# Sliding-window attention beside a gated GeLU block: bursts of maxima moved by a slot, and one gate/up tile moved from the attention's filler to the stage of seven products

## The chip, the cores and the metric

The kernel runs on one core of a Trainium2 chip. The metric is the device time of one execution in microseconds (us). Three runs of the kernel before gave 1066.36, 1067.74 and 1068.19 us, so the median is 1067.74. The profile shows one further execution.

## What is computed

The input x has 2048 tokens of 640 numbers. It is normalised, and two blocks read the result; both outputs are added to x. Everything is float32 at the interface.

```python
x = A_x
xn = _layernorm(x, axis=-1)
return x + _A_ref(xn, A_wqkv, A_wo) + _B_ref(xn, B_w_gate, B_w_up, B_w_down)
```

Block A is attention with 32 heads of 20 numbers. A query sees itself and the 255 keys ahead of it; softmax runs over those. Block B is `(gelu(xn @ w_gate) * (xn @ w_up)) @ w_down` with 1728 hidden columns.

## The kernel before

**Precision.** A dense product of float32 matrices is made of three products of a high and a low part (high by high, low by high, high by low). With 640 = 5 x 128 input rows, one 128x512 block of output takes 15 matrix products of 512 columns (`dense_steps`, L105).

**Stages.** They follow each other on TensorE: (1) layer norm, transposes and the first q/k and v projections; (2) the attention, in which TensorE fills the time between attention steps with projections, which the text calls the filler; (3) the gate/up products that the filler did not do, in pairs of token blocks with a scheme of seven products in place of eight (`gate_up_pair`, L935), ahead of them four plain blocks of the last, half-width tile (`gate_up`, L105 with tile `ps_g`); (4) the down and output projections (`terms`, L1202).

**Gate/up tiles.** The hidden columns are cut into 14 tiles (0 to 13) of 128 gate and 128 up columns; tile 13 has 64 of each. Tiles 0 to NFA-1 go through the filler (`gate_up_fill`): 4 token chunks of 512, a gate and an up block each, 15 products a block, so 120 products a tile. Tiles NFA to 12 go through `gate_up_pair`: a call does two of the four chunks of a tile with 6 + 9 + 6 + 9 + 6 + 9 + 9 = 54 products, so 108 products a tile. In both cases the result `he` is stored to DRAM as `hd`, from where stage 4 loads it.

**The attention's clock.** `attention()` walks through units u of four heads and 512 queries (32 units, and a 33rd turn for the last one's end). Each unit has NS = 14 slots, and in each slot the code writes down, in this order: actions that fell due (`tick`), two maxima (`pull_max`) in some slots, in slot 0 the weighted sum of values of the unit before (`av_unit`, L586, tile `ps_o`), in odd slots up to 11 two pieces of scores with their exponentials (`exp_piece`, matrix products L545 into `ps_e`, exponential L547 on ScalarE), and RATE/14 products of the filler (`pull_fill`; a v product of 320 columns counts 0.65). All engines but SyncE keep the order in which this is written.

**Maxima.** `max_pair` computes scores once more in another orientation, as 60x64 tiles of the array (L480, tile `ps_m`; 8 to 16 products for a pull of two), and VectorE takes the row maximum (L490, `junk`). Eight pairs make one unit's maxima: in the kernel before four in slot 0 (two ahead of `av_unit`, two behind it), two in slot 4 and two in slot 8; the first turn takes slot 2 for the second pair. MXD slots after a unit's last pair `max_end` transposes the maxima with one product (L507, `ps_n`), and a DMA writes them into rows of the queries, so that the scores come out with the maximum already taken off.

**After the scores.** GpSimd zeroes what lies outside the window in the exponentials P (`clear`, L558 and L561), then `av_unit` uses them. The scores have two PSUM buffers (tag "ex", which `av_unit` uses too), the maxima four ("mx"), the filler two ("dn"). P has three buffers a unit, called X, Z and Y in the order of their exponentials; `av_unit` reads X first, Y last.

**The filler's order** is the list `sets`: first the third and last chunk of q/k pair 0, then the sets one after the other, each with four chunks. A q/k chunk is saved by `save_qk` in steps on ScalarE (L265, L246), VectorE (L261) and GpSimd (L247), then stored to DRAM; a gate/up chunk takes five steps on ScalarE and VectorE and none on GpSimd. The weights of the next set are split into high and low on ScalarE (L622) and GpSimd (L627). When the slot number reaches V1_SLOT, the filler does the v projection of the upper 16 heads (`proj_v`, tile `ps_v`).

```python
sets = [("qk", 1), ("gu", 0), ("qk", 2), ("qk", 3), ("qk", 4)]
sets += [("gu", f) for f in range(1, NFA)] + [("gu", NF - 1)]
```

The filler does all of `sets` but the last; what is left when the slots end is done behind the last `av_unit`.

Of the kernel before, what the change touches and what calls it, by code (L numbers as in the profile page):

```python
# [28 lines left out]
SR = 3 * DH  # L29
QROWS = 64 + SR  # L30
NS = 14
RATE = 42.2
V1_SLOT = 158
MXD = 6
KSLOT = 9
LAG = 3, 5, 4, 4, 4, 4, 3, 3, 4, 3, 2, 1, 1, 1
NFA = 6
HD = D // 2
HR = 5
NQD = 9  # L40
# [25 lines left out]
def block_kernel(ctx, tc, x, wqk, wv, wgu, wdo, wdl, out):  # L66
# [131 lines left out]
    def at(slot, fn, *a):  # L198
        acts.setdefault(slot, []).append((fn, a))
# [9 lines left out]
    def flush():  # L209
        while lates:  # L210
            fn, a = lates.pop(0)
            fn(*a)
# [108 lines left out]
    def run(*gens):  # L321
        for gen in gens:
            for _ in gen:
                pass
# [121 lines left out]
    def load_stack(u, which=(0, 1)):  # L446
        g, c = divmod(u, NC)
        for m in range(80 * g // 128, (80 * g + 79) // 128 + 1):
            assert all((m + 5 * i, c) in done for i in which), (u, m)

        for i in which:
            dst, src, top, again = ((qs[u % NQ], qd[c], 1, 2), (ks[u % NK], kd[c], 0, 0))[i]
            for j in (0, 2):
                for p, part, n in ((j * 32, top, 2), (j * 32 + 2 * DH, again, 1), (64 - j * 32, 0, 3)):
                    nc.sync.dma_start(dst[p:p + DH * n, j:j + 2].rearrange("p j t -> p (j t)"),
                                      src[g, part:part + n].rearrange("s (d j) t -> (s d) (j t)",
                                                                      j=4)[:, j * C:(j + 2) * C])
# [73 lines left out]
    def exp_piece(u, s):  # L531
        g, c = divmod(u, NC)
        bi, j = divmod(s, 4)
        bank = pieces(c)[bi]
        q = qs[u % NQ]
        if j == 0:
            pts[u, bi] = ap.tile([128, 4, C], F32, name="P", tag="P", bufs=3)
        pt = pts[u, bi]
        lo = min(p[1] for p in bank)
        hi = max(p[1] + p[3] for p in bank)  # L540
        ps = psx.tile([128, C], F32, name="ps_e", tag="ex")
        for kb, col, q0, n in sorted(bank, key=lambda p: p[3]):
            k = ks[(u - (kb < 4 * c)) % NK]
            kc = kb % 4 * 128
            nc.tensor.matmul(ps[:, col:col + n], k[0:QROWS, j, kc:kc + 128], q[0:QROWS, j, q0:q0 + n],  # L545
                             start=True, stop=True)
        nc.scalar.activation(pt[:, j, lo:hi], ps[:, lo:hi], AF.Exp, scale=SCALE)  # L547
        if j == 3:
            defer(1, clear, u, bi)
# [56 lines left out]
    def load_gu(f):  # L606
        raws = []
        for i in range(2 if f < NF - 1 else 1):
            raw = wrp.tile([128, KT, 128], F32, name="wr", tag="wr")
            nc.sync.dma_start(raw, wgu[2 * f + i])  # L610
            raws.append(raw)
        return raws
# [4 lines left out]
    def split_later(pool, bufs, raw):  # L617
        hi = pool.tile([128, KT, 128], F32R, name="wqh", tag="wqh", bufs=bufs)
        lo = pool.tile([128, KT, 128], F32R, name="wql", tag="wql", bufs=bufs)

        def high():
            nc.scalar.activation(hi, raw, AF.Copy)  # L622
            for k in range(KT):
                defer(1 + k, low, k)

        def low(k):
            nc.gpsimd.tensor_tensor(out=lo[:, k], in0=raw[:, k], in1=hi[:, k].bitcast(F32), op=OP.subtract)  # L627

        defer(1, high)
        return hi, lo  # L630
# [37 lines left out]
                                   lambda k: xh[:, k, cs], lambda k: xl[:, k, cs], KT)  # L668
            defer(1, *((late, c4) if i else (c1,)))

    sets = [("qk", 1), ("gu", 0), ("qk", 2), ("qk", 3), ("qk", 4)]
    sets += [("gu", f) for f in range(1, NFA)] + [("gu", NF - 1)]
    pools = (wp, None), (hp, 2)
    rest = []

    def filler():
# [6 lines left out]
        for s, (kind, i) in enumerate(sets[:-1]):  # L683
            nxt = []
            after = sets[s + 1]
            for c in range(NC):
# [14 lines left out]
                if c in (1, 2) and c <= len(raws):  # L701
                    nxt.append(split_later(*pools[(s + 1) % 2], raws[c - 1]))
                if pending and now[0] >= V1_SLOT:
                    pending = False
# [8 lines left out]
    def x_sums(p, k, half):  # L713
        w = C // 2
        a, b = (slice((2 * p + i) * C + half * w, (2 * p + i) * C + half * w + w) for i in (0, 1))
        eh, el = xh.bitcast(F32), xl.bitcast(F32)
        live = {}

        def tile_of(i):
            live[i] = ap.tile([128, w], F32, name="tx", tag="tx")  # L720
            return live[i]

        def pool(o, i, j, op):
            nc.gpsimd.tensor_tensor(out=o, in0=i, in1=j, op=op)

        def store(i):
            t = live[i]
            defer(2, lambda: nc.sync.dma_start(td[p][i][:, k, half * w:half * w + w], t))

        def s1():  # L730
            pool(tile_of(1), eh[:, k, b], eh[:, k, a], OP.subtract)

        def s2():
            pool(live[1], live[1], el[:, k, b], OP.add)

        def s3():
            pool(live[1], live[1], el[:, k, a], OP.subtract)
            store(1)

        def s4():  # L740
            pool(tile_of(2), eh[:, k + 2, b], live[1], OP.subtract)

        def s5():
            pool(live[2], live[2], el[:, k + 2, b], OP.add)
            store(2)

        def s6():
            pool(tile_of(4), eh[:, k + 2, a], live[2], OP.subtract)

        def s7():  # L750
            pool(live[4], live[4], el[:, k + 2, a], OP.add)
            store(4)

        def s8():
            pool(tile_of(3), eh[:, k + 2, b], eh[:, k, b], OP.subtract)

        def s9():
            pool(live[3], live[3], el[:, k + 2, b], OP.add)

        def s10():  # L760
            pool(live[3], live[3], el[:, k, b], OP.subtract)
            store(3)

        return s1, s2, s3, s4, s5, s6, s7, s8, s9, s10
# [6 lines left out]
    def pull_max(n, slot):  # L771
        for _ in range(n):
            x = next(stream, None)
            if x is None:
                return
            max_pair(*x)
            if x[1] == 7:
                at(slot + (MXD if slot >= 0 else 4), max_end, x[0])

    def tick():  # L780
        todo = [y for t in sorted(t for t in acts if t <= now[0]) for y in acts.pop(t)]
        return sorted(todo, key=lambda y: y[0] is max_end)

    def pull_fill(n):
        debt[0] += n
        while debt[0] > 0:
            debt[0] -= next(fill, 1.0)

    def attention():
        now[0] = -1  # L790
        load_stack(0)
        load_stack(1)
        load_stack(2)
        for i, (p, k, half) in enumerate((p, k, half) for p in range(NC // 2) for k in range(2) for half in range(2)):
            for j, fn in enumerate(x_sums(p, k, half)):
                at(XS0 + XSN * i + 2 * j, fn)
        for i in range(12):
            now[0] = i - 13
            for fn, a in tick():
                fn(*a)  # L800
            if i % 2 == 0:
                pull_max(2, now[0])
            flush()
            pull_fill(2 * RAMP)
        pull_fill(GAP)
        for u in range(NU + 1):
            for i in range(NS):
                T = now[0] = NS * u + i
                for fn, a in tick():
                    fn(*a)  # L810
                if i in (0, 4, 8) or T == 2:
                    pull_max(2, T)
                if i == 0 and u:
                    av_unit(u - 1)
                    flush()
                    pull_max(2, T)
                if i % 2 and i < 12 and u < NU:
                    exp_piece(u, i - 1)
                    if i == 1 and u:
                        pull_fill(1)  # L820
                        debt[0] -= 1
                    exp_piece(u, i)
                flush()
                if u + 3 < NU and i in (KSLOT, 12):
                    load_stack(u + 3, (int(i == KSLOT),))
                pull_fill(RATE / NS)
        while acts:
            now[0] += 1
            for fn, a in tick():
                fn(*a)  # L830
            flush()
        now[0] = None
        run(fill)
        assert not acts
# [446 lines left out]
    order.__enter__()  # L1281
    raws_w = load_gu(NFA)
    banks = [psg.tile([128, C], F32, name="ps_g", tag=f"g{i}") for i in range(4)]
# [32 lines left out]

    raws_next = {NFA + 1: load_gu(NFA + 1)}
    for j, f in enumerate(range(NFA, NF - 1)):
        end = f + 1 == NF - 1
# [93 lines left out]
    for n, (p, k) in enumerate(steps):  # L1413
        i = n % (NQD + 1)
# [71 lines left out]
```

## Time and profile before

| what | value |
|---|---|
| the profiled execution's own time | 1067.07 us |
| its span, first to last instruction of the profile | 1065.2 us |
| median of three runs without a profile | 1067.74 us |
| TensorE busy | 1052.9 us, 99% of the span |
| VectorE, ScalarE, GpSimd busy | 68%, 50%, 35% |
| attention, first `av_unit` to last filler product | 108.5 to 637.9 us |
| plain blocks of tile 13 | 637.92 to 651.55 us |
| stage 3, 7 tiles, 756 products | 651.55 to 822.94 us |
| stage 4 | 822.94 to the end |

Times are counted from the first instruction of the profile. A row of the timeline gives the start, the length to the end of the last of the merged instructions, the engine, the line, the operation, the tiles (output first), the shape and the count; the bracket behind it is the idle time ahead and what ended it. Matrix products overlap, and their ends are modelled, so the text works with distances from start to start. PE is TensorE, PEld its weight loads, DVE VectorE, ACT ScalarE, POOL GpSimd, SP SyncE.

### The profile page before, as it was taken

Reading aid. Unit: us, or ns where it says so; the run is one execution under the profiler, and the core shown is the slowest. Engines: PE = TensorE matmul, PEld = TensorE weight load, DVE = VectorE, ACT = ScalarE, POOL = GpSimd, SP = SyncE. Lnnn points to the kernel's source line nnn. Section 1 sums busy time; section 2 is a strip of 40 time slices with the busy share of each in tenths; the row PEclk is TensorE's granted clock in tenths of the full one; section 3 lists DMA queues with packets and bytes.
Section 4 is the critical chain, followed back from the end, with each engine's and each line's share of the span. In section 5 each row is a group of like instructions: output and inputs, shape, how many; then the busy total and the mean of one; then the engine's idle time right before and its main releaser. Section 6 shows DMA issues by size and latency. Waiting matters only on the chain.

```text
span 1065.2 us, 25614 instructions
## 1 busy us (share of the span) xinstructions
PE 1052.9 (99%) x9429; PEld 832.7 (78%) x9429; DVE 722.9 (68%) x1985; ACT 531.1 (50%) x1120; POOL 375.6 (35%) x550
## 2 busy tenths in 40 slices
PE   8999999999999999999999999999999999999998
PEld 8877666666678766666666678888888999999998
DVE  7845656565554456666666627787776879888887
ACT  4434665566656565565656565332234543433332
POOL 6021665777764484746556351211100000000000
PEclk9999999999999999999999999999999999999999
DMA  5642344455452244424333215565766873343433
GB/s 196 187 150 75 105 148 131 137 141 176 135 157 81 84 143 122 147 90 139 99 105 123 66 63 199 173 247 204 251 247 247 277 254 129 128 134 103 133 129 105
DMA packets 105190, 158.74 MB, mean 149 GB/s; under 512 B 15420, under 2 KB 60092, under 8 KB 105064
## 3 DMA queue, kind: packets, MB, share of 16 engines
q1 hardware_dynamic: 102680, 150.95, 44.0%
q10 hardware_dynamic: 2384, 6.16, 1.7%
q8 instruction: 74, 1.21, 0.5%
q14 instruction: 52, 0.43, 0.1%
HBM read 101.78 MB, written 54.92 MB: 147 GB/s over the span
## 4 chain that ended last, share of the span: by engine, by line
PE 84%; DVE 5%; POOL 4%; DMA 3%; issue 2%; ACT 2%; SPq 0%; ACTq 0%; DVEq 0%; POOLq 0%
PE ps_d L105 25%; PE ps L1202 19%; PE ps_g L935 16%; PE ps_e L545 7%; PE ps_v L105 6%; PE ps_o L586 5%; PE ps_m L480 4%; PE ps_g L105 1%; POOL pt L247 1%; DVE junk L490 1%; DMA xi<-x 1%; POOL P L561 1%; POOL P L558 1%; DVE ss L1040 1%; DMA hr<-od 1%
## 5 line engine op out<-in xcount | busy, mean ns | idle before, releaser
L490 DVE CUSTOM_DVE_ANT_0 junk<-ps_m,mask 128x320 bf16<-128x320 f32 (+2 forms) x512 | 243.0, 475 | 171.7 <-PE ps_m L480 114.1
L547 ACT ACTIVATE P<-ps_e 128x512 f32<-128x512 f32 (+2 forms) x384 | 199.0, 572 | 106.3 <-PE ps_e L545 102.2
L1202 PE MATMUL ps<-wb,at 128*128 128x320 f32 x999 | 156.1, 309 | 0.3 <-DVE at L1040 0.3
L1202 PEld LDWEIGHTS ps<-wb,at 128*128 128x128 f32 x999 | 148.9, 188 | 0.8 <-DVE at L1040 0.6
L105 PE MATMUL ps_d<-xh,wql 128*128 128x512 f32 x430 | 136.7, 421 | 0.0
L105 PE MATMUL ps_d<-xh,wqh 128*128 128x512 f32 x430 | 135.1, 419 | 0.0
L105 PE MATMUL ps_d<-xl,wqh 128*128 128x512 f32 x430 | 134.8, 418 | 0.0
L545 PE MATMUL ps_e<-qs,ks 124*128 124x128 bf16 (+2 forms) x704 | 118.2, 279 | 0.3
L558 POOL TENSOR_SCALAR_AFFINE_SELECT P<-P 128x512 f32<-128x512 f32 x128 | 82.2, 642 | 101.9 <-ACT P L547 99.5
L545 PEld LDWEIGHTS <-ks 124*128 124x128 bf16 x704 | 48.6, 99 | 61.0 <-issue 48.6
L1202 PE MATMUL ps<-wt,at 128*128 128x320 f32 x552 | 89.2, 310 | 0.8 <-DVE xr L1225 0.8
L105 PEld LDWEIGHTS ps_d<-xl,wqh 128*128 128x128 f32 x430 | 77.4, 189 | 15.4 <-issue 3.4
L105 PEld LDWEIGHTS ps_d<-xh,wql 128*128 128x128 f32 x430 | 77.0, 189 | 15.7 <-issue 3.6
L105 PEld LDWEIGHTS ps_d<-xh,wqh 128*128 128x128 f32 x430 | 76.7, 189 | 15.5 <-issue 3.1
L1202 PEld LDWEIGHTS ps<-wt,at 128*128 128x128 f32 x552 | 82.9, 188 | 1.3 <-DVE xr L1225 1.0
L561 POOL TENSOR_SCALAR_AFFINE_SELECT P<-P 128x512 f32<-128x512 f32 x112 | 70.8, 642 | 35.4 <-ACT P L547 35.4
L1156 ACT ACTIVATE at<-ss 128x512 fp32r<-128x512 f32 x59 | 37.3, 633 | 88.5 <-DVE ss L1040 88.5
L586 PE MATMUL ps_o<-P,v 64*32 64x320 f32 (+4 forms) x2816 | 75.9, 348 | 0.9 <-POOL P L561 0.6
L247 POOL TENSOR_TENSOR pt<-r,pt 128x512 bf16<-128x512 f32 x40 | 46.5, 1164 | 77.1 <-ACT pt L246 73.7
L586 PEld LDWEIGHTS ps_o<-P,v 64*32 64x32 f32 x2816 | 48.5, 106 | 26.6 <-POOL P L558 3.4
L480 PE MATMUL ps_m<-ks,qs 60*64 60x320 bf16 (+3 forms) x1472 | 63.3, 260 | 2.6 <-DVE xl L192 1.1
L480 PEld LDWEIGHTS <-qs 60*64 60x64 bf16 x1472 | 28.3, 105 | 42.1 <-issue 36.7
(195 smaller groups left out, 1754.0 us busy)
## 6 DMA issues: line engine op xcount, KB each, us to landing
hr<-hd SPq DMA_DIRECT2D x104, 128.0 KB
hd<-he SPq DMA_DIRECT2D x50, 256.0 KB
wr<-wgu SPq DMA_DIRECT2D x27, 320.0 KB
qs<-qd SPq DMA_DIRECT2D x64, 120.0 KB
ks<-kd SPq DMA_DIRECT2D x64, 120.0 KB
xi<-x SPq DMA_DIRECT2D x16, 320.0 KB
qs<-qd SPq DMA_DIRECT2D x64, 80.0 KB
ks<-kd SPq DMA_DIRECT2D x64, 80.0 KB
```

The lines of the kernel that those rows point to most:

```text
L105: nc.tensor.matmul(ps, a(k), b(k), start=n == 0, stop=n == 3 * nk - 1)
L247: nc.gpsimd.tensor_tensor(out=pt[:, l, :], in0=r, in1=pt[:, 1, :], op=OP.subtract)
L480: nc.tensor.matmul(ps[64 * h:64 * h + 64, col:col + w], q[rows, j, q0:q0 + 64], ks_, start=True, stop=True, tile_position=(64 * r, 64 * h))
L490: nc.vector.tensor_tensor_reduce(out=junk[:, 0:n], in0=ps[:, 320 - n:320], in1=mask[:, 320 - n:320], scale=1.0, scalar=NEG, op0=OP.add, op ...
L545: nc.tensor.matmul(ps[:, col:col + n], k[0:QROWS, j, kc:kc + 128], q[0:QROWS, j, q0:q0 + n], start=True, stop=True)
L547: nc.scalar.activation(pt[:, j, lo:hi], ps[:, lo:hi], AF.Exp, scale=SCALE)
L558: nc.gpsimd.affine_select(out=a, in_=a, pattern=[[0, 4], [1, 128]], compare_op=OP.is_ge, fill=0.0, base=0, channel_multiplier=-1)
L561: nc.gpsimd.affine_select(out=a, in_=a, pattern=[[0, 4], [-1, 128]], compare_op=OP.is_ge, fill=0.0, base=-1, channel_multiplier=1)
L586: nc.tensor.matmul(os[r][32 * j:32 * j + 32, qa:qb], v[rows, w0_:w0_ + 32], pt[rows, j, col + qa - q0:col + qb - q0], start=r not in begun ...
L935: nc.tensor.matmul(ps, i, j, start=first and n == 0, stop=n == len(work) - 1, skip_group_check=True)
L1156: nc.scalar.activation(hi[:, 3:7], s, AF.Copy)
L1202: nc.tensor.matmul(ps[bank][:, 0:HD], *work[bank][j], start=bank not in begun, stop=final[p, bank] == n and j == len(work[bank]) - 1, skip ...
```

## The change

NFA goes from 6 to 5, so tile 5 goes through `gate_up_pair` and no longer through the filler; RATE, the filler products of a unit, goes from 42.2 to 38.8. The pulls of maxima in slots 4 and 8 move to slots 5 and 9 (in the first turn 2 to 3), which are slots with scores; MXD goes from 6 to 7, so `max_end` also falls into a slot with scores. In the list of sets q/k pairs 2 and 3 go ahead of gate/up tile 0. V1_SLOT goes from 158 to 169.

```diff
-RATE = 42.2
-V1_SLOT = 158
-MXD = 6
+RATE = 38.8
+V1_SLOT = 169
+MXD = 7
-NFA = 6
+NFA = 5
-    sets = [("qk", 1), ("gu", 0), ("qk", 2), ("qk", 3), ("qk", 4)]
+    sets = [("qk", 1), ("qk", 2), ("qk", 3), ("gu", 0), ("qk", 4)]
-                if i in (0, 4, 8) or T == 2:
+                if i in (0, 5, 9) or T == 3:
                     pull_max(2, T)
```

The first place is TensorE in a unit in the middle of the attention, around the second pull of maxima. L480 are the maxima, L105 with `ps_d` the filler, L545 the scores. Before:

```order
L480 LDWEIGHTS qs_184
L480 MATMUL ps_m<-ks_188,qs_184 64x256
L105 MATMUL ps_d<-xh_77,wql 128x512 x3
L545 LDWEIGHTS ks_185
L545 MATMUL ps_e<-qs_182,ks_185 128x256
```

and with the change:

```order
L480 LDWEIGHTS qs_184
L480 MATMUL ps_m<-ks_188,qs_184 64x256
L545 LDWEIGHTS ks_185
L545 MATMUL ps_e<-qs_182,ks_185 128x256
L545 LDWEIGHTS ks_186
```

The three filler products between maxima and scores are gone from there; they stand ahead of the maxima now. Over the whole program 92 runs of filler stood between maxima and scores, and 31 do now.

The second place is a little further in the same unit, TensorE around the transposed maxima (L507). Before:

```order
L105 MATMUL ps_d<-xh_77,wql 128x512
L105 MATMUL ps_d<-xl_81,wqh 128x512 x2
L507 LDWEIGHTS nm_189
L507 MATMUL ps_n<-identb,nm_189 128x128
L105 MATMUL ps_d<-xl_81,wqh 128x512 x3
L545 LDWEIGHTS ks_185
L545 MATMUL ps_e<-qs_182,ks_185 128x256
```

and with the change:

```order
L105 MATMUL ps_d<-xh_76,wql 128x512 x2
L105 MATMUL ps_d<-xl_80,wqh 128x512 x3
L507 LDWEIGHTS nm_189
L507 MATMUL ps_n<-identb,nm_189 128x128
L545 LDWEIGHTS ks_185
L545 MATMUL ps_e<-qs_182,ks_185 128x256
```

Here the filler behind the transpose has moved ahead of it: of 30 runs of filler between L507 and scores, one is left.

The third place is the end of the attention on TensorE: the last scores (L545) and the last `av_unit` (L586). Before:

```order
L545 LDWEIGHTS ks_188
L545 MATMUL ps_e<-qs_183,ks_188 128x384
L105 MATMUL ps_d<-xh_79,wql 128x512 x5
L105 MATMUL ps_d<-xl_83,wqh 128x512 x4
L586 MATMUL ps_o<-P,v 32x320 x8
L586 MATMUL ps_o<-P,v 32x256 x8
```

and with the change:

```order
L545 LDWEIGHTS ks_188
L545 MATMUL ps_e<-qs_183,ks_188 128x384
L586 MATMUL ps_o<-P,v 32x320 x8
L586 MATMUL ps_o<-P,v 32x256 x8
L586 MATMUL ps_o<-P,v 32x192 x8
```

The nine filler products that stood between them are gone: the filler's last four products now stand ahead of the last four score products, and one that stood behind `av_unit` is gone too.

## The prediction

> **What bounds the kernel now.** I read the page first, then the stages (busy time in seven stretches), then the chain of work that ended last.
>
> ```profile
> PE 1052.9 (99%) x9429; PEld 832.7 (78%) x9429; DVE 722.9 (68%) x1985; ACT 531.1 (50%) x1120; POOL 375.6 (35%) x550
> PEclk9999999999999999999999999999999999999999
> 108.50:299.28 190.78, 189.00 (x2191) 121.55 (x2188) 114.74 (x410) 118.52 (x236) 131.49 (x191) 1.00 0.47 138
> 366.81:604.49 237.68, 237.00 (x2777) 155.47 (x2774) 152.31 (x533) 141.27 (x283) 139.72 (x215) 1.00 0.38 117
> 651.55:822.94 171.39, 171.39 (x759) 141.91 (x758) 127.62 (x212) 55.78 (x103) 17.88 (x12) 1.00 0.64 224
> ```
>
> The stretches give the length, then busy time and count of PE, PEld, DVE, ACT and POOL, then the granted clock. TensorE is busy nearly all the time at full clock; the nearest other engine in the attention is POOL with 131.49 of 190.78 us early, DVE with 152.31 of 237.68 late. So TensorE's own work sets the time, and the question is what each product and each change between kinds of products costs on it.
>
> The two stretches of the attention start at an `av_unit` each and hold 11 and 14 units: 17.34 and 16.98 us a unit. The early units are 0.36 us longer, where POOL is busier (69% against 59%), so there are small stalls there now, some 4 us in all. In stage 3 DVE is busy 127.62 of 171.39 us and PE never waits.
>
> The chain gives clean prices for a filler product and a product of stage 3:
>
> ```profile
> 415.06 2.07 PE ps_d L105 x9
> 651.55 171.39 PE ps_g L935 x756
> ```
>
> That is 0.230 us for a filler product and 0.2267 for one of stage 3. The ends are modelled, so what a change of kind costs I take from starts, in one undisturbed stretch of a unit (PE alone, in order of time):
>
> ```profile
> 424.06 0.47 PE L480 MATMUL ps_m<-ks,qs 60*64 60x256 bf16 x16
> 424.46 0.96 PE L105 MATMUL ps_d<-xh,wqh 128*128 128x512 f32 x3
> 425.27 0.61 PE L545 MATMUL ps_e<-qs,ks 124*128 124x256 bf16 x4
> 425.63 0.95 PE L105 MATMUL ps_d<-xh,wql 128*128 128x512 f32 x3
> 426.42 0.23 PE L507 MATMUL ps_n<-identb,nm 128*128 128x128 bf16 x1
> 426.46 0.70 PE L105 MATMUL ps_d<-xh,wql 128*128 128x512 f32 x2
> 427.00 0.40 PE L105 MATMUL ps_d<-xl,wqh 128*128 128x512 f32 x1
> 427.24 0.61 PE L545 MATMUL ps_e<-qs,ks 124*128 124x256 bf16 x4
> 427.61 0.93 PE L105 MATMUL ps_d<-xl,wqh 128*128 128x512 f32 x3
> 428.47 0.47 PE L480 MATMUL ps_m<-ks,qs 60*64 60x320 bf16 x8
> ```
>
> Three filler products are worth 0.69 us. From maxima to scores they took 425.27 - 424.46 = 0.81, so that run costs 0.12 us beyond its products. From the transposed maxima to scores: 427.24 - 426.46 = 0.78, so 0.09. From scores to maxima: 428.47 - 427.61 = 0.86, so 0.17. Each separate run of filler costs about 0.1 us; fewer, longer runs do the same products in less time.
>
> **The change part by part.**
>
> *Tile 5 leaves the filler.* 120 products x 0.230 = 27.6 us less, if TensorE stays the bound. Its weight splits, and the five steps on ACT and DVE of each of its four chunks, leave the attention with it.
>
> *Tile 5 enters stage 3.* Two calls of 54 products = 108 x 0.2267 = 24.5 us more. DVE's share there, 74%, also holds side jobs that do not grow with the tiles, so I add no wait; a wait per call would show as a length above 12.24 us (54 x 0.2267). The two parts together give -3.1 us.
>
> *Maxima directly ahead of scores.* 61 runs of filler between them go (92 to 31); their products join other runs. If scores behind maxima cost what they cost behind filler, each saves 0.12: 61 x 0.12 = 7.3 us. The trace has no scores directly behind maxima, so I bound it. At best the whole 0.17 of the dearest change of kind goes: 10.4 us. At worst the scores pay for coming from a 60x64 tiling what maxima pay more than scores for being entered, 0.17 - 0.12 = 0.05, and save nothing: 3 us lost. I take 7.3, since the nearest row, maxima followed by filler, shows no surcharge against the run behind the transpose (0.12 against 0.09).
>
> [...]
>
> *The transposed maxima ahead of scores.* 29 runs x 0.09 = 2.6 us, by the same rows; bounds 0 and 29 x 0.12 = 3.5. MXD is one slot later, so its DMA has 8 slots in place of 9 until the scores of the next unit; at 16.98 / 14 = 1.21 us a slot and a little less with the change, that is still 9 us, so I cost it at nothing.
>
> *The end of the attention.* Here the order has no filler left between the last scores and the last `av_unit`. Now:
>
> ```profile
> 632.06 0.61 ACT L640 ACTIVATE gs<-ps_d 128x512 f32<-128x512 f32 x1
> 632.44 0.61 PE L545 MATMUL ps_e<-qs,ks 124*128 124x128 bf16 x4
> 632.54 0.62 ACT L641 ACTIVATE he<-ps_d 128x512 f32<-128x512 f32 x1
> 633.01 1.13 ACT L547 ACTIVATE P<-ps_e 128x512 f32<-128x512 f32 x2
> 634.27 0.63 POOL L558 TENSOR_SCALAR_AFFINE_SELECT P<-P 128x512 f32<-128x512 f32 x1 [2.67 <-ACT P L547]
> 634.85 0.63 POOL L561 TENSOR_SCALAR_AFFINE_SELECT P<-P 128x512 f32<-128x512 f32 x1
> 635.05 2.45 PE L586 MATMUL ps_o<-P,v 64*32 64x320 f32 x96
> 635.44 0.63 POOL L558 TENSOR_SCALAR_AFFINE_SELECT P<-P 128x512 f32<-128x512 f32 x1
> ```
>
> From the last scores (632.44) to the second zeroing's end (635.48) are 3.0 us, to the third's 3.6. Now nine filler products cover that. With the change `av_unit` can start some 0.4 us behind the scores and gets to buffer Y half way, 1.2 us later, so it waits 3.0 - 1.6 = 1.4 us for Y. I add 1.5 us; bounds 0.8 (no gate steps ahead of the exponentials on ACT) and 2.0 (all of the third).
>
> *Less cover a unit.* RATE takes 3.4 products = 0.78 us from a unit, the merged runs another 2 x 0.12 + 0.09 = 0.33: a unit falls from 16.98 to about 15.9 us. What ACT and POOL do for a unit stays, but for tile 5's share. In the early stretch POOL did 131.49 / 11 = 12.0 us a unit, ACT 10.8, DVE 10.4: all fit into 15.9, on average. But pairs of scores now come with five products between some of them: 0.36 (425.27 to 425.63) + 5 x 0.23 + 0.13 = 1.6 us, where two exponentials take 1.13 and any other step on ACT 0.6. Such a pair may wait a few tenths for its PSUM buffer. And q/k pairs 2 and 3, whose chunks each put a low part on POOL, come without the gate tile between them. I add 2.5 us of new stalls; bounds 0 and 6 (half as much again as the 4 us of now, for the units' tighter fit). DVE's merged work is not larger; a burst of two pairs keeps four slots of 1.14 us at least until the next.
>
> *V1_SLOT and the order of sets* move the same products; 11 slots later is some 12 us later for a v projection whose 240 products take the same time wherever they stand. Nothing, except through POOL above.
>
> **The sum:** -27.6 + 24.5 - 7.3 - 2.6 + 1.5 + 2.5 = -9.0 us. The profiled execution took 1067.07 us (span 1065.2 and 1.9 around it), so 1058.1 by its own time. It lies 0.67 us under the median of the runs shown; carried to the median, **1058.7 us**.
>
> **The rivals.**
>
> *The changes of kind cost the same in the new order*, because scores behind maxima pay what filler behind maxima paid: the 7.3 us do not come, the rest does. -9.0 + 7.3 = -1.7, so 1066.0; with no new stalls 1063.5. For it: maxima are the only ones in another tiling, and going to them is the dearest change (0.17). Against: filler behind them costs hardly more than elsewhere. [...]
>
> *ScalarE becomes the bound between scores.* With 1.6 us for a pair and one other step of 0.6 us in front of two exponentials (1.13), the pair is 0.1 us late, with two steps 0.7. If three pairs a unit lose 0.1, 31 units lose 9 us in place of the 2.5 that I have: 1065.2. For it: the last quoted scores waited 0.57 us for ACT to start. Against: ACT is busy 59% late and has slots 12, 13 and 0 to catch up.
>
> *GpSimd becomes the bound, and the kernel is slower.* In the early stretch `av_unit` needs P zeroed in time; POOL works in order, and q/k low parts, weight splits and the sums for stage 3 stand between. If POOL cannot follow at 15.9 us a unit, the first 11 units keep their 17.34 and the saving of 1.1 us + 0.36 each is lost: 16 us in place of the 2.5: 1058.7 + 13.5 = 1072.2. It decides from the point where POOL's work from one `av_unit` to the next passes 15.9 us. Against: 12.0 us a unit now.
>
> *The tile does not save in stage 3.* If each of the two calls met a wait as long as its six saved products (1.4 us), the first two parts give 0 in place of -3.1: 1061.8. Against: no wait in the 14 calls of now.
>
> **How the numbers follow.** The sum as worked out, with its stalls between 0 and 6: 0.62, for 1055 to 1062. The changes of kind cost the same: 0.16, for 1063.5 to 1066. ScalarE: 0.13, for 1062 to 1066. POOL, slower: 0.05. No saving in stage 3: 0.04, inside the first range. The best bound of the maxima's part without new stalls gives 1053; the range, 1054 to 1065, leaves out that edge, POOL, and the worst of the second and third cases. This kernel's measurement tells 0.2% (2.1 us) from no change. Faster by more than that is all below 1065.6: 0.62 + 0.04 + most of the second and third, 0.85. Within 0.2%: 0.09. Slower: 0.06.
>
> **What would show it.** In the changed kernel's timeline the distance from a burst of maxima to the filler behind the scores, at 16 maxima and 4 scores, should be 0.40 + 0.36; 0.12 more means the second case. Units late in the attention should be 15.9 us from `av_unit` to `av_unit`; 16.3 and idle time of PE released by P on ACT means the third. Early units over 16.5 us with `av_unit` released by POOL mean the fourth. Stage 3 should take 864 x 0.2267 = 195.9 us, and the last `av_unit` should show about 1.5 us of waiting on POOL. The prediction is wrong at its root if TensorE's length of a unit does not follow its own products.

## The result, and the profile after

The changed kernel takes 1060.68 us in the median of 4 runs (1058.85 to 1063.06), the kernel before 1067.77 beside it. The ratio is 0.9933, 95% interval 0.991 to 0.9957: 7.1 us faster. The forecast was 1058.7, so the direction held and the gain is 2.0 us smaller. The interval of the measurement is 1058.2 to 1063.2 us, so 2.0 us lie inside it: where they went is read from the traces below, not from the times. The profiled execution of the changed kernel took 1058.85 us, the fastest of the four; part of that is luck, which the last section takes out.

The page and the stages of the changed kernel, in the columns of before (the same units early and late, then stage 3 and stage 4):

```profile
PE 1037.7 (98%) x9417; PEld 833.4 (79%) x9417; DVE 729.1 (69%) x1996; ACT 530.0 (50%) x1120; POOL 374.5 (35%) x542
105.38:287.06 181.68, 176.50 (x2155) 117.02 (x2151) 110.75 (x406) 117.04 (x233) 131.69 (x193) 1.00 0.50 149
349.71:572.39 222.68, 221.59 (x2736) 150.18 (x2732) 147.20 (x524) 137.86 (x283) 138.81 (x207) 1.00 0.40 121
617.74:813.61 195.87, 195.87 (x866) 162.21 (x865) 141.47 (x235) 62.62 (x116) 20.88 (x14) 1.00 0.58 201
813.61:1057.10 243.49, 238.49 (x1616) 236.79 (x1614) 204.75 (x441) 99.84 (x179) 0.00 (x0) 1.00 0.48 157
```

Late in the attention a unit takes 222.68 / 14 = 15.91 us, where the prediction said 15.9. Stage 3 takes 195.87 us, where it said 195.9. The early units are another matter: 181.68 / 11 = 16.52 us, 0.61 over the late ones, and TensorE is idle for 5.2 of the 181.68 us, where before it was idle for 1.8 of 190.78.

The heart of the forecast was the price of a change of kind, and the trace now shows what it could not before: scores directly behind maxima, and directly behind the transposed maxima (TensorE alone, a unit late in the attention):

```profile
499.88 0.47 PE L480 MATMUL ps_m<-ks,qs 60*64 60x256 bf16 x16
500.28 0.61 PE L545 MATMUL ps_e<-qs,ks 124*128 124x256 bf16 x4
500.65 0.94 PE L105 MATMUL ps_d<-xh,wql 128*128 128x512 f32 x3
501.43 0.84 PE L105 MATMUL ps_d<-xl,wqh 128*128 128x512 f32 x3
502.12 0.23 PE L507 MATMUL ps_n<-identb,nm 128*128 128x128 bf16 x1
502.18 0.60 PE L545 MATMUL ps_e<-qs,ks 124*128 124x256 bf16 x4
502.54 0.71 PE L105 MATMUL ps_d<-xl,wqh 128*128 128x512 f32 x2
503.09 0.86 PE L105 MATMUL ps_d<-xh,wqh 128*128 128x512 f32 x3
503.88 0.47 PE L480 MATMUL ps_m<-ks,qs 60*64 60x320 bf16 x8
```

From maxima to scores 0.40 us, from scores to filler 0.37: the 16 maxima take what they took ahead of filler, and the four scores what they took behind filler (0.36). Nothing is paid for the new neighbours; behind the transposed maxima it is 0.06 us to the scores, 0.04 to the filler before. The run of filler that stood between them is gone with its 0.12 us; its products are in the runs of six and five, at 1.47 us for six (0.09 beyond 1.38). Why a run of its own costs about 0.1 us is not settled by these rows. The weight loads give a hint: ahead of these scores they stand idle for 0.27 us behind filler (at 425.26 in before), and not at all behind the 16 maxima (500.28), but for 0.25 again behind the eight (504.27).

### The profile page after: what moved, and what is told of

Its sections match the earlier page's. It is cut to its first block, busy times and chain, and to the rows that moved or that the text cites. A ratio compares the mean times of both kernels' runs of the same rounds, so it can differ in the third digit from the quotient of the medians.

```text
span 1057.1 us, 25607 instructions
## 1 busy us (share of the span) xinstructions
PE 1037.7 (98%) x9417; PEld 833.4 (79%) x9417; DVE 729.1 (69%) x1996; ACT 530.0 (50%) x1120; POOL 374.5 (35%) x542
## 4 chain that ended last, share of the span: by engine, by line
PE 79%; DVE 7%; POOL 4%; DMA 4%; issue 3%; ACT 2%; SPq 1%; ACTq 0%; DVEq 0%; POOLq 0%
PE ps_d L105 21%; PE ps_g L935 17%; PE ps L1202 16%; PE ps_e L545 7%; PE ps_v L105 6%; PE ps_o L586 5%; PE ps_m L480 4%; DVE junk L490 1%; PE ps_g L105 1%; POOL pt L247 1%; POOL tx L724 1%; POOL P L561 1%; POOL P L558 1%; DMA hr<-hd 1%; ACT P L547 1%
## 5 line engine op out<-in xcount | busy, mean ns | idle before, releaser
L105 PE MATMUL ps_d<-xh,wqh 128*128 128x512 f32 x390 | 119.8, 416 | 0.0
L105 PE MATMUL ps_d<-xl,wqh 128*128 128x512 f32 x390 | 119.7, 415 | 0.0
L105 PE MATMUL ps_d<-xh,wql 128*128 128x512 f32 x390 | 119.2, 415 | 0.0
L558 POOL TENSOR_SCALAR_AFFINE_SELECT P<-P 128x512 f32<-128x512 f32 x128 | 84.9, 663 | 92.9 <-ACT P L547 89.2
L545 PE MATMUL ps_e<-qs,ks 124*128 124x128 bf16 (+2 forms) x704 | 117.5, 278 | 0.1
L545 PEld LDWEIGHTS <-ks 124*128 124x128 bf16 x704 | 49.4, 98 | 49.1 <-issue 36.1
L586 PE MATMUL ps_o<-P,v 64*32 64x320 f32 (+4 forms) x2816 | 76.7, 348 | 5.3 <-POOL P L561 4.6
L105 PEld LDWEIGHTS ps_d<-xh,wql 128*128 128x128 f32 x390 | 71.0, 189 | 13.5 <-issue 1.6
L105 PEld LDWEIGHTS ps_d<-xl,wqh 128*128 128x128 f32 x390 | 71.1, 189 | 13.1 <-issue 1.4
L105 PEld LDWEIGHTS ps_d<-xh,wqh 128*128 128x128 f32 x390 | 70.5, 189 | 13.0 <-issue 1.6
L561 POOL TENSOR_SCALAR_AFFINE_SELECT P<-P 128x512 f32<-128x512 f32 x112 | 70.9, 644 | 23.6 <-ACT P L547 23.6
L586 PEld LDWEIGHTS ps_o<-P,v 64*32 64x32 f32 x2816 | 48.1, 106 | 31.9 <-POOL P L561 8.1
L98 POOL TENSOR_TENSOR wql<-wr,wqh 128x640 fp32r<-128x640 f32 x10 | 16.1, 1610 | 152.6 <-PE ps_g L935 128.0
L480 PE MATMUL ps_m<-ks,qs 60*64 60x320 bf16 (+3 forms) x1472 | 62.3, 260 | 3.6 <-DVE xl L192 1.1
```

The costliest lines, as they stand in the source:

```text
L105: nc.tensor.matmul(ps, a(k), b(k), start=n == 0, stop=n == 3 * nk - 1)
L480: nc.tensor.matmul(ps[64 * h:64 * h + 64, col:col + w], q[rows, j, q0:q0 + 64], ks_, start=True, stop=True, tile_position=(64 * r, 64 * h))
L558: nc.gpsimd.affine_select(out=a, in_=a, pattern=[[0, 4], [1, 128]], compare_op=OP.is_ge, fill=0.0, base=0, channel_multiplier=-1)
L561: nc.gpsimd.affine_select(out=a, in_=a, pattern=[[0, 4], [-1, 128]], compare_op=OP.is_ge, fill=0.0, base=-1, channel_multiplier=1)
L586: nc.tensor.matmul(os[r][32 * j:32 * j + 32, qa:qb], v[rows, w0_:w0_ + 32], pt[rows, j, col + qa - q0:col + qb - q0], start=r not in begun ...
```

## The experiments

All ratios are to the kernel before, timed on the same chip beside each group (median 1067.77 us beside the change, 1068.72 beside the next four kernels, 1068.02 beside the last four). The last two columns are lengths in us in the profiled execution.

| kernel | ratio | 95% interval | median us | early 11 units | late 14 units |
|---|---|---|---|---|---|
| the change | 0.9933 | 0.991 to 0.9957 | 1060.68 | 181.68 | 222.68 |
| moved bursts alone | 0.9921 | 0.9904 to 0.9938 | 1059.95 | 187.92 | 233.27 |
| moved tile alone | 1.0021 | 1.0006 to 1.0035 | 1070.63 | 183.85 | 227.63 |
| the change, old order of sets | 0.9911 | 0.9895 to 0.9928 | 1058.51 | 178.82 | 223.17 |
| the change, RATE 38.4 | 0.9926 | 0.9907 to 0.9946 | 1060.26 | 182.21 | 223.01 |
| the change, later sums | 0.9902 | 0.9881 to 0.9923 | 1058.09 | 178.84 | 222.71 |
| the change, MXD 6 | 0.997 | 0.9956 to 0.9983 | 1064.85 | 183.75 | 224.36 |
| later sums and RATE 38.4 | 0.9883 | 0.9861 to 0.9906 | 1056.17 | 176.48 | 222.71 |
| moved bursts alone, later sums | 0.9918 | 0.9896 to 0.994 | 1060.01 | 187.07 | 233.97 |

**Moved bursts alone.** The kernel before with

```diff
-MXD = 6
+MXD = 7
-                if i in (0, 4, 8) or T == 2:
+                if i in (0, 5, 9) or T == 3:
```

> The kernel before with only the bursts moved (slots 0, 5, 9, first turn 3; MXD 7); six tiles in the filler, old order of sets. If TensorE pays for every run of filler that stands by itself: 61 x 0.12 + 29 x 0.09 = 9.9 us less than before, less some new stalls of 0 to 2 us, so 1058 to 1060. If scores behind maxima pay what filler behind maxima paid (the rival): at most 2.6 us less, 1065 to 1068, and the run of 4 scores behind maxima is over 0.40 us long from start to start.

Measured 1059.95 us, 8.4 us less by the ratio (6.6 to 10.3 by its interval). In its trace four scores behind 16 maxima take 0.36 us from start to start (485.84 to 486.20). Its late units:

```profile
361.79:595.06 233.27, 232.59 (x2777) 159.13 (x2774) 152.00 (x533) 141.19 (x283) 139.82 (x215) 1.00 0.39 118
```

233.27 against 237.68 us with the same 2777 products in both, and the same 0.68 us of idle TensorE: 4.41 / 14 = 0.315 us a unit for the same work in another order. Two runs at 0.12 and one at 0.09 make 0.33. The rival, that scores behind maxima pay what filler there paid, falls.

**Moved tile alone.** The kernel before with

```diff
-RATE = 42.2
-V1_SLOT = 158
+RATE = 38.8
+V1_SLOT = 169
-NFA = 6
+NFA = 5
```

> The kernel before with only the tile moved (NFA 5, RATE 38.8, V1_SLOT 169); bursts in slots 0, 4, 8, old order of sets. If the gain comes from the changes of kind: 120 x 0.230 - 108 x 0.2267 = 3.1 us less, about 2 us back at the attention's end where the filler has run out, and 0 to 2 us of new stalls: 1065.5 to 1068.5. If the tile's move carries the gain: about 1061.

Measured 1070.63 us, ratio 1.0021, interval 1.0006 to 1.0035: by itself the tile's move costs 2.2 us. That is above the 1065.5 to 1068.5 us that were expected, so the waits had been put too low here. In the old schedule the whole gain, and a little more, comes from the bursts. Most of what eats the 3.1 us of saved products and 2.2 more shows in its list of waits (in total, times, longest):

```profile
PE ps_o L586 <- POOL P L561: 3.4, 6, 0.8
...
PE ps_e L545 <- ACT P L547: 0.9, 2, 0.5
...
PE ps_o L586 <- ACT P L547: 0.6, 1, 0.6
```

Before, the first of these was 0.6 us, once:

```profile
PE ps_o L586 <- POOL P L561: 0.6, 1, 0.6
```

Of these 4.9 us, 3.5 fall into the early units (GpSimd 2.6, ScalarE 0.9) and 0.9 on the attention's end. The early units became 0.63 us shorter each (183.85 against 190.78 us for 11), but GpSimd's work in them hardly shrank (129.24 against 131.49 us).

**The order of sets.** The changed kernel with the old list:

```diff
-    sets = [("qk", 1), ("qk", 2), ("qk", 3), ("gu", 0), ("qk", 4)]
+    sets = [("qk", 1), ("gu", 0), ("qk", 2), ("qk", 3), ("qk", 4)]
```

> The changed kernel with the old order of sets (q/k 1, gate/up 0, q/k 2, 3, 4). In the changed kernel's trace av_unit waits for GpSimd's zeroing some 3.8 us in its units 1 to 7, before some 0.8. If the new order of sets makes these waits (q/k low parts close together on GpSimd): 2 to 3 us under the changed kernel, 1057.5 to 1059. If the shorter units make them: as the changed kernel, 1060 to 1062.

Measured 1058.51 us, ratio 0.9911 against 0.9933 for the change; the intervals overlap. The traces point the same way: the late units stay within 0.5 us, the early ones are 2.9 us shorter, and TensorE is idle in them for 3.1 us in place of 5.2:

```profile
108.31:287.13 178.82, 175.69 (x2154) 117.00 (x2151) 111.81 (x407) 116.25 (x231) 130.07 (x190) 1.00 0.49 142
```

In these early units `av_unit` waits 2.8 us for GpSimd in place of 3.8, and the waits for loads (0.8 us) are gone. So the new order costs some 2 to 3 us early, but explains only part of the waits for GpSimd.

**RATE 38.4.** The changed kernel with filler left for the end:

```diff
-RATE = 38.8
+RATE = 38.4
```

> The changed kernel with RATE 38.4 in place of 38.8, so that 8 products of filler stand between the last scores and the last av_unit again, and 3 behind it. If the wait at the attention's end is a lack of cover: 1.5 to 2.5 us under the changed kernel (whose median is 1060.7), 1058 to 1059.5. If it is set by ScalarE and GpSimd whatever TensorE does there: no difference, 1060 to 1061.5.

Measured 1060.26 us, no difference that can be told from the change. That is what was expected of an end that ScalarE and GpSimd set, but the trace shows another reason, and both halves of it are in its list of waits (here with the loads):

```profile
PE ps_o L586 <- POOL P L561: 5.0, 8, 1.1
...
PE ps_m L480 <- DMA qs<-qd: 1.2, 2, 0.7
```

The wait at the attention's end has gone, but of the waits of `av_unit` for GpSimd there are 5.0 us in place of 4.6, all but 0.2 of them before the late units, and the loads of q for the maxima are late by 1.2 in place of 0.8. In the early units 0.4 x 11 x 0.23 = 1.0 us of filler is taken away, and yet they take 182.21 us in place of 181.68. TensorE is idle there for 6.8 us in place of 5.2. Where an early unit waits for GpSimd anyway, less filler only makes the wait longer: by the trace, what the end gained was given back ahead of it.

**Later sums.** That should be so only as long as GpSimd is crowded. The sums for stage 3 (L724, 80 steps of about 0.74 us) can start later:

```diff
-XS0, XSN = 24, 50
+XS0, XSN = 122, 36
```

> The changed kernel with the sums for stage 3 on GpSimd (L724, eight groups of 10) started at slot 122 and every 36 slots, in place of slot 24 and every 50, so that none falls into the units with q/k pairs 2 and 3. By the rows' lengths GpSimd then has at most 15.3 us of work in any unit, where the changed kernel has 17.2 in unit 4. If the early waits of av_unit are GpSimd's crowding: the 3.8 us of them in units 1 to 7 go, 1057 to 1058.5. If they come from the shorter units as such, whatever GpSimd has to do: as the changed kernel, 1060 to 1061.5.

Measured 1058.09 us, ratio 0.9902; its interval overlaps with that of the change (0.9933), so the gain of 3.3 us is better shown by the trace. Of the 80 steps 15 in place of 30 now fall into the early units:

```profile
107.02:285.86 178.84, 176.57 (x2154) 117.19 (x2151) 110.73 (x406) 116.95 (x233) 120.98 (x177) 1.00 0.49 145
```

GpSimd has 120.98 us of work there in place of 131.69, TensorE is idle for 2.3 us in place of 5.2, and `av_unit` waits for GpSimd 2.1 us in all:

```profile
PE ps_o L586 <- POOL P L561: 2.1, 6, 0.5
```

The late units are as long as in the change, though GpSimd has 146.18 us of work there now in place of 138.81: it is not how much it does in all that matters. Counted from one `av_unit` to the next, GpSimd is busy for 15.3 to 16.4 us in three early units of the change, and these last 16.9 to 17.7 us; with later sums no early unit has more than 14.1. The amount in one unit does not decide alone: a late unit of this kernel has 15.2 us of work in place of 12.5 and is as long as in the change (16.3 us). What stands ahead of the zeroing there was not resolved.

**MXD 6.** The changed kernel with the transposed maxima back in a slot without scores:

```diff
-MXD = 7
+MXD = 6
```

> The changed kernel with MXD 6 in place of 7: the transposed maxima stand in a slot without scores again, with filler on both sides. If each of the 29 runs of filler behind them costs 0.09: 2.6 us over the changed kernel, 1063 to 1064. If what the runs cost was filled by waits anyway: as the changed kernel, 1060 to 1061.5.

Measured 1064.85 us, ratio 0.997 against 0.9933: 3.9 us, where 2.6 were expected; the intervals touch at their ends (0.9956 and 0.9957). The late units:

```profile
352.22:576.58 224.36, 222.88 (x2736) 148.77 (x2732) 146.76 (x524) 138.24 (x283) 138.53 (x207) 1.00 0.40 121
```

They are 1.68 us longer than in the change, 0.12 a unit. Of that 0.39 us is more idle TensorE; its busy time grows by 222.88 - 221.59 = 1.29 us, 0.09 a unit, which is the price that the run was given. The early 11 units are 2.1 us longer, with 1.0 us of new waits of the scores for the exponentials, so the slot also matters to ScalarE. So the run costs what it was priced at, 2.6 us over 29, and the rest of the 3.9 is new waits or noise.

**Later sums and RATE 38.4 together.** Both edits above in the changed kernel.

> The changed kernel with the later sums and RATE 38.4 (filler between the last scores and the last av_unit). If both causes are right, the early waits and the wait at the end go: 1055.5 to 1057.5. If RATE gives nothing, as between the changed kernel and the one with RATE 38.4 alone (1060.7 and 1060.3): as the run with later sums.

Measured 1056.17 us, ratio 0.9883, the best of all: 5.3 us under the change by the ratios. With GpSimd relieved, RATE gives what it did not give alone: 2.0 us by the ratios of the two kernels with later sums, 0.9902 and 0.9883. The intervals of these two overlap, so the end of the attention is better shown by the traces. With the change (scores, exponentials, zeroing, last `av_unit`, first plain block):

```profile
599.41 0.61 PE L545 MATMUL ps_e<-qs,ks 124*128 124x128 bf16 x4
599.84 1.08 ACT L547 ACTIVATE P<-ps_e 128x512 f32<-128x512 f32 x2
600.58 1.89 PE L586 MATMUL ps_o<-P,v 64*32 64x320 f32 x48 [0.56 <-ACT P L547]
601.05 0.87 POOL L558 TENSOR_SCALAR_AFFINE_SELECT P<-P 128x512 f32<-128x512 f32 x1 [1.56 <-ACT P L547]
601.88 0.81 POOL L561 TENSOR_SCALAR_AFFINE_SELECT P<-P 128x512 f32<-128x512 f32 x1
602.74 1.33 PE L586 MATMUL ps_o<-P,v 64*32 64x320 f32 x48 [0.27 <-POOL P L561]
604.01 1.43 PE L105 MATMUL ps_g<-xh,wqh 128*128 128x512 f32 x5
```

and with both edits, where eight filler products stand between:

```profile
595.27 0.61 PE L545 MATMUL ps_e<-qs,ks 124*128 124x128 bf16 x4
...
597.65 2.45 PE L586 MATMUL ps_o<-P,v 64*32 64x320 f32 x96
...
600.03 0.96 PE L105 MATMUL ps_d<-xl,wqh 128*128 128x512 f32 x3
```

In the first, 4.60 us pass from the last scores to the next product, for 0.32 + 2.38 = 2.7 us of work: 1.9 us of nothing. In the second 4.76 us pass: 0.31 for the scores, 2.07 for the run of eight (8 x 0.23 and 0.23 for the change of kind, as much as the run of nine ahead of the last `av_unit` paid before, 632.75 to 635.05) and 2.38 for `av_unit`. No wait is left.

**Moved bursts alone, later sums.** The kernel before with the bursts and the sums moved.

> The kernel before with the moved bursts alone, and the later sums: six tiles in the filler, old order of sets. Its units are 0.8 us longer than the changed kernel's, so fewer waits are to be had: 0 to 1.5 us under the run with moved bursts alone (ratio 0.9921 to before), 1058 to 1060. It says whether the tile's move pays once GpSimd is not crowded: if it does, the run with both is 2 to 3 us lower than this.

Measured 1060.01 us, ratio 0.9918: as the bursts alone (0.9921). With units 0.8 us longer GpSimd was not late to begin with. The run with later sums and RATE 38.4, which has the tile's move (and the new order of sets) beside the bursts, is at 0.9883: 3.7 us less, where the saved products were put at 3.1. The intervals of the ratios overlap a little (0.9861 to 0.9906 and 0.9896 to 0.994), but the two were timed beside the same runs of before, and of their eleven times only one of the first (1058.29) lies above the lowest of the second (1058.01). So the tile's move does pay, once its two side effects are cured.

## Why the prediction was right, point by point

- **What bounds the kernel.** TensorE, in the order of its products, as said. It follows in every kernel from the late units: 16.98 us before, 16.66 with the bursts, 16.26 with the tile, 15.91 with both; 0.315 and 0.72 make 1.03, and 1.07 was measured. The 4 us of small stalls that the prediction saw in the early units of before were not all stalls: TensorE was idle there for 1.8 us.
- **Tile 5 leaves the filler** (-27.6). The late units lose 0.72 us with the tile alone, where 0.78 was said; 0.04 of the rest are new waits.
- **Tile 5 enters stage 3** (+24.5). Measured 195.87 - 171.39 = 24.48, without a wait.
- **Maxima and transposed maxima ahead of scores** (-7.3 and -2.6). Together 0.315 us a late unit in place of 0.33. By the times it is 8.4 us with the bursts alone, where these two make 9.9, which is inside the interval of 6.6 to 10.3. The transposed part alone is the 0.09 us of work a unit that it was priced at.
- **The end of the attention** (+1.5). 1.9 us without work. The reason was named rightly; that `av_unit` would also wait for ScalarE at its start (0.56 us) was not in it. With the wait for the zeroing (0.27 us) that is 0.83 us by the brackets; the 1.9 us are counted from start to start.
- **New stalls** (+2.5). This is the term that was too small, in part for a cause that the prediction named without a price of its own: q/k pairs 2 and 3 without the gate tile between them. By the stretches TensorE's idle time goes from 1.8 to 5.2 us early and from 0.7 to 1.1 us late: 3.8 us. `av_unit` waits 4.6 us for GpSimd in place of 0.6, 3.8 of it early and 0.3 in the end above, and the maxima wait 0.8 us for loads, which did not happen before. From the list of waits of the change:

```profile
PE ps_o L586 <- POOL P L561: 4.6, 7, 1.5
...
PE ps_m L480 <- DMA qs<-qd: 0.8, 2, 0.4
```

- **The rivals.** Changes of kind that cost the same: refuted by the rows above. The 60*64 maxima pass to 124*128 scores in the 0.40 us that they take ahead of filler (499.88 to 500.28 with the change, 424.06 to 424.46 before). Since products of another tiling follow the maxima in both orders (128*128 before, 124*128 with the change), the rows cannot say what a change of tiling costs by itself. Nor are the maxima the only products in another tiling, as the prediction had it: those of `av_unit` stand as 64*32 in every timeline. ScalarE between scores: in the change no score product waits for it in the list of waits; only `av_unit` does, at the attention's end. Of the 0.57 us that the prediction quoted for this rival, 0.43 pass between scores and exponential also where ScalarE stands ready (617.44 to 617.87 before, ScalarE idle for the 0.46 us ahead). GpSimd: the mechanism is there, in the early units, at 3.4 us of added idle time in place of the 16 of that rival. The tile that does not save: so it is by itself (+2.2 us), but not by waits in stage 3, where that rival looked for them; it loses them in the attention.

The parts by themselves, -8.4 and +2.2, make -6.2 us. The kernel with just these two moves is the one with the old order of sets, and it has -9.5 by its ratio; the change, with the new order, has -7.1. So the two moves are worth 3.3 us more together than one by one, about as much as the intervals of the three ratios leave open. By the traces 2.2 us of it lie in the early units: the bursts take 2.86 us from them, the tile 6.93, both 11.96. Why is not shown.

What stays open is why stage 4, whose products the change does not touch, took 242.4 us in the profile of before (from its first product) and between 242.8 and 245.3 in the others, 243.5 in the change. In the longest, that with MXD 6, TensorE waits there 2.2 us for VectorE (L1040), before 0.3. It may hold another 1 us of the difference to the forecast, and no run here tests it.

## What to carry to other kernels

When one engine is busy all the time, look at the order of its work: a run of filler between two kinds of small products cost 0.12 us here, and putting the small products side by side gained 8 us without taking out any. When a change shortens a repeated unit, list the work of the other engines unit by unit, since the mean hides the crowded one: GpSimd was busy 72% of the early stretch and still late, and moving 15 of its steps out of that stretch took 2.9 us of idle time from TensorE there, nearly as much as the tile's saved products are worth (3.1). A filler should last until the last wait that it covers, but leaving more of it for the end pays only where nothing else sets the pace ahead of it: here it gave 2.0 us by the ratios with GpSimd relieved, and without that no difference that can be told.

## What the runs showed of the hardware that was not expected

Runs of one kernel lay several us apart, in the change from 1058.85 to 1063.06, in 17 runs of the kernel before from 1063.78 to 1071.81, and one cause is in the traces. The stretch from 14 to 22 us in the profile of before (the granted clock is the number behind POOL's):

```profile
14.00:22.00 8.00, 8.00 (x57) 8.00 (x56) 4.99 (x15) 2.37 (x6) 5.93 (x7) 0.79 0.25 87
```

and in that of the change:

```profile
14.00:22.00 8.00, 8.00 (x68) 8.00 (x67) 6.39 (x19) 3.17 (x8) 6.79 (x8) 1.00 0.26 87
```

The program is the same there. From 14 to 17 us the granted clock of before is 0.50, and a mean of 0.79 over 8 us is 3.4 us at half clock, 11 products fewer, about 1.7 us lost. The kernel with the bursts alone has such a stretch from 61 to 73 us instead:

```profile
61.00:73.00 12.00, 10.89 (x63) 8.30 (x62) 5.62 (x20) 3.80 (x7) 3.65 (x4) 0.86 0.63 187
```

That is 0.14 x 12 = 1.7 us again. Both places have TensorE waiting for steps of the layer norm on VectorE just ahead (0.7 us ahead of the first in before, 1.1 us ahead of the second). Of the ten profiled executions four (granted clock 1.000 or 0.999) have none, four (0.998) one and two (0.997 and 0.996) both, so a single run of this kernel is uncertain by up to 3.4 us for this alone. The granted clock that is noted with every run says the same: of the 34 runs of the kernel before beside the experiments, the eight at 1.000 take 1066.6 us in the mean, the thirteen at 0.998 take 1068.3 and the eight at 0.997 take 1069.7. What lets the clock fall is not shown: in the 6 us ahead of the first stretch (8 to 14 us) TensorE was busy for 4.32 us in the profile of before and for 4.31 in that of the change, and the clock fell in one and not in the other. Taking out the 1.7 us that the profile of before lost and that of the change did not, their 8.2 us of difference become 6.5, on the other side of the 7.1 of the medians.
